# Loading the first block of a gated attention and feed-forward kernel: x tile by x tile, with the value products in the order of arrival

## The chip, the core and the metric

The kernel runs on one core of one Trainium2 chip. TensorE multiplies matrices (it loads a stationary operand, then streams a moving one), VectorE and ScalarE do the element work and empty PSUM, GpSimd writes constants, and SyncE (SP) issues most DMAs; ScalarE (ACT) issues two. The metric is the device time of one execution in microseconds (us), as the median of several runs. A profile of one execution gives the times inside it, counted from its first instruction (the span).

## The reference

```python
x = A_x                                                  # [1, 2048, 640], bf16
g = sigmoid((x * gate_w).sum(-1, keepdims=True))
# A: linear attention, 32 heads of 20
q, k, v = split_heads(x @ wqkv)                          # wqkv [640, 1920]
phi(t) = concat(softmax(t @ w_phi), softmax(-(t @ w_phi)))   # w_phi [32, 20, 20], per head
kv = phi(k)^T v ;  z = sum over tokens of phi(k)
a = (phi(q) kv / (phi(q) z + 1e-6)) @ wo                 # wo [640, 640]
# B: feed-forward
b = (gelu(x @ w_gate) * (x @ w_up)) @ w_down             # F = 1728
out = g * a + (1 - g) * b
```

## The kernel before, in words

The 2048 tokens are 16 tiles of 128; four tiles make a block. The 640 features are five slices (`KD = 5`) of 128 rows, which TensorE needs on the partitions, so everything begins with x transposed: `xT` holds it. Tiles 4 to 15 are transposed by DMA on their way in (`xturn`, L236). The first block goes another way, since it is wanted first: its tokens are loaded as they lie (`xload`, L229; tile j takes every fourth token, and two tiles come in one DMA of 320 KB), transposed on TensorE in 64-row halves through the identity (`x_transpose`, L333, with the transposes at L342), and copied out of PSUM into `xT` (L350 to L355: half of tile 3 on ScalarE and half on VectorE; tiles 0 and 2 whole on VectorE; tile 1 whole on ScalarE).

`attention_state` (L670) writes the order of work out by hand. It begins with nine products of constants (L674), warm-up that needs no data. Then come the transposes of tiles 0 and 1, six small filler products (L682), the transposes of tiles 2 and 3, and the values of the first block: `v_step(t, kt)` (L473) adds slice kt's share to the values of tile t, 640 columns in two products (480 in bank t, 160 in bank 4 or 5). For slice 0 the weights come in two DMAs (columns 0 to 255, then the rest; `VA = 256`), and the products are split in the same way. Slices 1 to 3 follow, each for all four tiles; then the block diagonals, the gate column, and slice 4, after which each tile's values are copied into `vaug` (`v_first_evac`, L484).

`blockdiag` (L357) spreads w_phi over `BD` in five VectorE instructions (L361); `BD` is later the moving operand of `fold` (L385), which multiplies w_phi into the key weights `wkT` and the query weights `wqT`. `gate_column` (L367) transposes the gate row `gz` on TensorE (L370) and VectorE copies it beside the value weights (L372); the first product that reads it is the second part of `v_tile(4, 2)`.

After the first values, three chunks of the up projection of block 0 are computed ahead (`up_ahead`, L546, products at L464), then the values of tiles 4 and 5, `fold` for the keys, the values of tiles 6 and 7, the keys of tile 0, two more up chunks, `fold` for the queries, and a loop over the tiles. The feed-forward part follows (`ffn`, L949).

The order of loads is fixed in `loads` (L222). SP issues, one after another: two x pairs, the value weights (two DMAs for slice 0, one of 160 KB for each further slice), the up weights of three chunks (`wue`, 480 KB), the DMA transposes of x tiles 4 and 5, of `wkT`, of x tiles 6 and 7, two more up chunks (`wul`), `wqT`, and x tiles 8 to 15 in two. ScalarE issues w_phi (25 KB, L276) after the second of GpSimd's masks, and the gate row (1.2 KB, L279). A helper, `_Sched`, sets the waits: an operation waits for the last writer of each tile it reads and for the readers of each it overwrites. Each engine works in program order.

Of the kernel before, what the change touches and what calls it, by code (L numbers as in the profile page):

```python
# [3 lines left out]
P = 128  # L4
BF16 = mybir.dt.bfloat16
F32 = mybir.dt.float32
AF = mybir.ActivationFunctionType
# [100 lines left out]
class _Kernel:  # L108
    S, D, H, DH, F = 2048, 640, 32, 20, 1728
    KD = D // P  # L110
# [111 lines left out]
    def loads(self):  # L222
        sc, nc = self.sc, self.nc
        D, KD, DH, P_ = self.D, self.KD, self.DH, P
        w3 = self.wqkv.rearrange("(kt p) n -> p kt n", p=P)

        x4 = self.x[0:self.BT, :].rearrange("(p j) n -> p j n", j=self.TB)

        def xload(q, j):  # L229
            sc.dma(q, lambda e: e.dma_start(self.xtok[:, j:j + 2, :], x4[:, j:j + 2, :]),  # L230
                   writes=[("xtok", j), ("xtok", j + 1)])

        def wload(T, c0, key):
            sc.dma("sp", lambda e: e.dma_start_transpose(T[:, :, :], self.wqkv[:, c0:c0 + D]), writes=[key])
# [1 line left out]
        def xturn(t, n):  # L236
# [5 lines left out]
              writes=["gtmp"])  # L242
        sc.op("pool", lambda e: e.memset(self.ident[:, :], 0.0), writes=["ident"])
        sc.op("pool", lambda e: e.affine_select(self.ident[:, :], self.ident[:, :], pattern=[[-1, P]],
                                                compare_op=ALU.not_equal, fill=1.0, base=0, channel_multiplier=1),
              writes=["ident"])
        xload("sp", 0)
        xload("sp", 2)
        for kt in range(KD):
            for a, z, key in ((0, self.VA, ("wv", 0)), (self.VA, D, "wv0")) if kt == 0 else ((0, D, ("wv", kt)),):  # L250
                sc.dma("sp", lambda e: e.dma_start(self.w3[:, kt, a:z], w3[:, kt, 2 * D + a:2 * D + z]), writes=[key])  # L251
        u3 = self.wu.rearrange("(kt p) n -> p kt n", p=P)
        a, z = self.UP[0] * P, 7 * P
        sc.dma("sp", lambda e: e.dma_start(self.wu_sb[:, :, a:z], u3[:, :, a:z]), writes=["wue"])
# [4 lines left out]
               writes=["wul"])  # L259
# [5 lines left out]
        for i in range(KD):  # L265
            n = self.HHI[i] - self.HLO[i] + 1
# [6 lines left out]
            pool(lambda e, m=m, n=n, base=base: e.affine_select(  # L273
                m, m, pattern=[[DH, n]], compare_op=ALU.is_ge, fill=0.0, base=DH - 1 - base, channel_multiplier=-1),
                [("mask", i)])
        sc.dma("act", lambda e: e.dma_start(  # L276
            self.wphi_sb[:, :, :], self.wphi.rearrange("h d f -> (h d) f").rearrange("(i p) f -> p i f", p=P)),
            reads=[("mask", 1)], writes=["wphi"])
        sc.dma("act", lambda e: e.dma_start(self.gz[0:KD, :], self.gw.rearrange("(k p) -> k p", p=P)), writes=["gz"])  # L279
        for r in (0, 1):  # L280
            m = self.hmask[:, r, :]
            pool(lambda e, m=m: e.memset(m, 1.0), [("hmask", r)])
# [47 lines left out]
            self.load(self.wd_sb[64 * r:64 * r + 64, 13, :], self.wd[13 * P:self.F, :], ("wd13", r))  # L330
        self.load(self.wo_sb[:, :, :], self.wo.rearrange("(kt p) n -> p kt n", p=P), "wo")

    def x_transpose(self, t, ek):  # L333

        sc = self.sc
        b, w = (0, 4, 2, 6)[t], self.D // 2
        bks = (b, b + 1)
        pv = self.bank(b, 1024).bitcast(BF16).rearrange("p (r c) -> p r c", r=2)[:, :, 0:w]
        for c in range(self.KD):
            for r in (0, 1):  # L340
                a = 64 * r
                sc.op("pe", lambda e: e.transpose(  # L342
                    pv[:, r, c * 64:(c + 1) * 64], self.xtok[a:a + 64, t, c * P:(c + 1) * P],
                    self.ident[a:a + 64, a:a + 64]),
                    reads=[("xtok", t), "ident"], writes=[("ps", bks[r])], signal=(c == self.KD - 1))
        out = self.xT[:, :, t * P:(t + 1) * P].rearrange("p c (r t) -> p c r t", t=64)
        src = pv.rearrange("p r (c t) -> p c r t", t=64)
        rd = [("ps", b) for b in bks]
        if ek == "ad":
            sc.op("act", lambda e: e.activation(out[:, :, 0, :], src[:, :, 0, :], AF.Copy), reads=rd[:1], writes=[("xh", t)])  # L350
            sc.op("dve", lambda e: e.tensor_copy(out[:, :, 1, :], src[:, :, 1, :]), reads=rd[1:], writes=[("xT", t)])
        elif ek == "a":
            sc.op("act", lambda e: e.activation(out, src, AF.Copy), reads=rd, writes=[("xT", t)])
        else:
            sc.op("dve", lambda e: e.tensor_copy(out, src), reads=rd, writes=[("xT", t)])  # L355

    def blockdiag(self):  # L357
        DH = self.DH
# [114 lines left out]
    def v_step(self, t, kt, part=None):  # L473
        sc = self.sc
        tail = (480, 160, 4 + t // 3, 160 * (t % 3))
        parts = ([(0, self.VA, t, 0)], [(self.VA, 480 - self.VA, t, self.VA), tail], [(0, 480, t, 0), tail])
        for c0, n, bk, col in parts[2 if part is None else part]:
            sc.op("pe", lambda e, c0=c0, n=n, bk=bk, col=col: e.matmul(  # L478
                self.bank(bk)[:, col:col + n], self.xT[:, kt, t * P:(t + 1) * P], self.w3[:, kt, c0:c0 + n],
                start=(kt == 0 and col == 0), stop=(kt == self.KD - 1), skip_group_check=True),  # L480
                reads=[("xT", t), ("xh", t), "wv0" if part == 1 else ("wv", kt)], writes=[("ps", bk)],
                signal=(kt == self.KD - 1))

    def v_first_evac(self, ts, ek, tail):  # L484
        sv, nt = ts[0], len(ts)
# [184 lines left out]
    def attention_state(self):  # L670
        NT = self.NT
        sc = self.sc
        ones = self.nc.const_aps.tensor(1.0, [P, 512], BF16)
        for n in (512, 512, 512, 512, 512, 512, 128, 128, 128):  # L674
            sc.op("pe", lambda e: e.matmul(self.bank(0, n), ones[:, 0:P], ones[:, 0:n], start=True, stop=True),
                  writes=[("ps", 0)])
        vs, ve, xt = self.v_step, self.v_first_evac, self.x_transpose
        xt(0, "d")
        xt(1, "a")
        for i in range(3):  # L680
            for a, b in ((0, 2), (64, 3)):
                sc.op("pe", lambda e: e.matmul(self.bank(b, P), ones[a:a + 64, 0:P], ones[a:a + 64, 0:P], start=True,  # L682
                                               stop=True), writes=[("ps", b)])
        xt(2, "d")
        xt(3, "ad")
        for t, part in ((0, 0), (1, 0), (0, 1), (1, 1), (2, 0), (2, 1), (3, 0), (3, 1)):
            vs(t, 0, part)
        for kt in range(1, 4):
            for t in range(4):
                vs(t, kt)  # L690
        self.blockdiag()
        self.gate_column(6)
        for t in range(4):
            vs(t, 4)
            ve([t], "ad"[t % 2], False)
            if t == 2:
                ve([0, 1, 2], "a", True)
        ve([3], "d", True)
        v, k, q = self.v_tile, self.k_tile, self.q_tile
        self.up_ahead(0, 7, "d")  # L700
        self.up_ahead(1, 6, "a")
        self.up_ahead(2, 4, "d")
        v(4, 2)
        self.v_split(5, 0)
        m, t, p = "main", "tail", "strip"
# [333 lines left out]
```

## Time and profile before

| what | value |
|---|---|
| median of 3 runs | 283.37 us (283.24 to 283.39) |
| span of the profiled execution | 282.4 us |
| TensorE busy | 278.6 us (99% of the span) |
| VectorE, ScalarE, GpSimd busy | 173.2, 105.9, 15.1 us |
| granted TensorE clock over the span | 1.000 |
| first transposes of x (L342) | 3.99 us |
| first value products (L478) | 5.37 us |
| first ahead-of-time up product (L464) | 11.53 us |

The time of a run is taken around the whole execution, while the span is from its first instruction to its last: the median stands 0.97 us above the span, and this difference is carried along. Busy time of TensorE counts pipelined products, whose ends are modelled. The chain that ended last is followed back from the last instruction: at each step to what released it, or to the instruction before it on its engine. "issue" is time in which an engine waited for nothing that the profile shows. In a timeline, neighbouring instructions of a line are merged into one row (start, length, engine, line, operation, output and inputs, count), and a bracket names the idle time ahead of them and what ended it; SPq and ACTq rows are DMA issues.

### The profile page before, as it was taken

Reading aid. Unit: us, or ns where it says so; the run is one execution under the profiler, and the core shown is the slowest. Engines: PE = TensorE matmul, PEld = TensorE weight load, DVE = VectorE, ACT = ScalarE, POOL = GpSimd, SP = SyncE. Lnnn points to the kernel's source line nnn. Section 1 sums busy time; section 2 is a strip of 40 time slices with the busy share of each in tenths; the row PEclk is TensorE's granted clock in tenths of the full one; section 3 lists DMA queues with packets and bytes.
Section 4 is the critical chain, followed back from the end, with each engine's and each line's share of the span. In section 5 each row is a group of like instructions: output and inputs, shape, how many; then the busy total and the mean of one; then the engine's idle time right before and its main releaser. Section 6 shows DMA issues by size and latency. Waiting matters only on the chain.

```text
span 282.4 us, 6904 instructions
## 1 busy us (share of the span) xinstructions
PE 278.6 (99%) x2926; PEld 168.6 (60%) x2926; DVE 173.2 (61%) x329; ACT 105.9 (38%) x204; POOL 15.1 (5%) x69
## 2 busy tenths in 40 slices
PE   7999999999999999999999999999999999999996
PEld 4566766665665444444444444445777777777786
DVE  1456999999997523694333324235883883883801
ACT  3246978777793332223232232321112112112011
POOL 7511001101000000000000000000000000000000
PEclk9999999999999999999999999999999999999999
DMA  7999169787789910011000000000133132532221
GB/s 213 193 223 190 29 127 172 153 175 149 157 175 274 350 51 0 2 24 23 2 0 0 0 2 0 0 0 2 26 50 98 46 49 78 66 49 73 73 72 49
DMA packets 60378, 24.11 MB, mean 85 GB/s; under 512 B 51002, under 2 KB 59834, under 8 KB 60346
## 3 DMA queue, kind: packets, MB, share of 16 engines
q1 hardware_dynamic: 59680, 23.63, 38.9%
q8 instruction: 23, 0.38, 0.6%
q10 hardware_dynamic: 666, 0.03, 0.2%
q14 instruction: 9, 0.07, 0.1%
HBM read 9.04 MB, written 2.62 MB: 41 GB/s over the span
## 4 chain that ended last, share of the span: by engine, by line
PE 97%; DMA 1%; SPq 0%; ACT 0%; issue 0%
PE ps L464 58%; PE ps L898 29%; PE ps L599 4%; PE ps L817 2%; PE ps L478 2%; PE ps L637 2%; DMA w<-in_A_wqkv_dram 1%; PE ps L404 1%; SPq L230 0%; SPq L251 0%; ACT outsb L911 0%; PE ps L370 0%
## 5 line engine op out<-in xcount | busy, mean ns | idle before, releaser
L464 PE MATMUL ps<-xT,wu_sb 128*128 128x512 bf16 x260 | 64.1, 379 | 0.0
L464 PE MATMUL ps<-xT,wg_sb 128*128 128x512 bf16 x260 | 63.9, 379 | 0.0
L779 ACT ACTIVATE gl<-ps 128x512 bf16<-128x512 f32 x52 | 31.0, 597 | 70.3 <-PE ps L464 70.3
L464 PE MATMUL ps<-w,xT 128*128 128x362 bf16 (+5 forms) x340 | 51.4, 302 | 0.0
L898 PE MATMUL ps<-wd_sb,hT 64*128 64x320 bf16 x648 | 48.4, 296 | 0.0
L781 DVE TENSOR_TENSOR hT<-ps,gl 128x512 bf16<-128x512 f32 x34 | 23.4, 689 | 37.7 <-PE ps L464 37.7
L464 PEld LDWEIGHTS ps<-xT,wu_sb 128*128 128x128 bf16 x260 | 25.4, 98 | 30.3 <-DVE hT L781 0.2
L464 PEld LDWEIGHTS ps<-xT,wg_sb 128*128 128x128 bf16 x260 | 25.1, 98 | 29.8 <-issue 0.2
L911 ACT ACTIVATE outsb<-ps,Gm 128x320 bf16<-128x320 f32 (+2 forms) x31 | 14.5, 515 | 71.8 <-PE ps L898 71.8
L464 PEld LDWEIGHTS ps<-w,xT 128*128 128x128 bf16 x340 | 31.9, 97 | 14.8
L898 PEld LDWEIGHTS ps<-wd_sb,hT 64*128 64x128 bf16 x648 | 30.9, 94 | 12.2 <-issue 0.4
L898 PE MATMUL ps<-wo_sb,goT 64*128 64x320 bf16 (+2 forms) x340 | 26.5, 288 | 0.0
L617 DVE TENSOR_REDUCE Dk<-Ek 128x66 f32<-128x1320 bf16 x16 | 24.3, 1520 | 2.3 <-ACT gcol L528 2.3
L626 DVE TENSOR_TENSOR Ek<-Ek,Dk 128x1320 bf16<-128x1320 bf16 x16 | 24.5, 1532 | 0.5
L863 DVE TENSOR_TENSOR O<-ps,RH 128x640 bf16<-128x640 f32 x32 | 24.7, 815 | 0.0
L538 ACT ACTIVATE Ek<-ps 128x627 bf16<-128x627 f32 x32 | 20.5, 693 | 6.4 <-PE ps L599 4.9
L538 ACT ACTIVATE Eqt<-ps 128x627 bf16<-128x627 f32 x32 | 20.6, 705 | 2.5 <-PE ps L464 2.5
L781 DVE TENSOR_TENSOR xT<-ps,gl 128x512 bf16<-128x512 f32 x13 | 9.0, 690 | 18.2 <-PE ps L464 18.2
L898 PEld LDWEIGHTS ps<-wo_sb,goT 64*128 64x128 bf16 x340 | 15.9, 94 | 5.3
L898 PE MATMUL ps<-wd_sb,xT 64*128 64x320 bf16 (+2 forms) x270 | 16.0, 269 | 0.0
L851 DVE RECIPROCAL RH<-ps 128x32 f32<-128x32 f32 x16 | 5.7, 357 | 14.4 <-PE ps L817 14.3
L898 PEld LDWEIGHTS ps<-wd_sb,xT 64*128 64x128 bf16 x270 | 12.1, 94 | 2.7
(90 smaller groups left out, 184.1 us busy)
## 6 DMA issues: line engine op xcount, KB each, us to landing
out_dram<-outsb SPq DMA_DIRECT2D x7, 320.0 KB, 2.3
wd_sb<-in_B_w_down_dram SPq DMA_DIRECT2D x1, 2080.0 KB, 11.0
wg_sb<-in_B_w_gate_dram SPq DMA_DIRECT2D x5, 224.0 KB, 3.1
wg_sb<-in_B_w_gate_dram SPq DMA_DIRECT2D x5, 192.0 KB, 3.5
wu_sb<-in_B_w_up_dram SPq DMA_DIRECT2D x5, 192.0 KB, 3.9
wo_sb<-in_A_wo_dram SPq DMA_DIRECT2D x1, 800.0 KB, 9.7
xtok<-in_A_x_dram SPq DMA_DIRECT2D x2, 320.0 KB, 3.3
w<-in_A_wqkv_dram SPq DMA_DIRECT2D x4, 160.0 KB, 4.0
```

The source lines that it names most:

```text
L464: self.sc.op("pe", lambda e: e.matmul(self.ps[:, bank * 512 + c0:bank * 512 + c0 + n], lhs, rhs, start=first, stop=fin), reads=reads, writ ...
L478: sc.op("pe", lambda e, c0=c0, n=n, bk=bk, col=col: e.matmul(self.bank(bk)[:, col:col + n], self.xT[:, kt, t * P:(t + 1) * P], self.w3[:, ...
L538: self.sc.op("act", lambda e: e.activation(dst, src, AF.Exp, scale=scale), reads=[("ps", b), ("ps", b + 1)], writes=[(name, sl, s)])
L599: self.sc.op("pe", lambda e: e.matmul(out, self.xT[:, kt, t * P:(t + 1) * P], self.w3[:, kt, c:c + 2 * n].rearrange("p (r w) -> p r w", w= ...
L617: self.sc.op("dve", lambda e: e.tensor_reduce(self.Dk[:, se, 0, :].rearrange("p (u h) -> p u h", h=self.HG), self.k_view(se), AX.X, ALU.ad ...
L626: sc.op("dve", lambda e: e.tensor_tensor(v, v, R.rearrange("p (u h) -> p u h", h=self.HG).unsqueeze(3).to_broadcast([P, 2 * self.G, self.H ...
L779: sc.op("act", lambda e: e.activation(self.gl[:, slot, :], self.bank(banks[0]), AF.Gelu_apprx_tanh), reads=[("ps", banks[0])], writes=[("g ...
L781: sc.op("dve", lambda e: e.tensor_tensor(hT, up, self.gl[:, slot, :], ALU.mult), reads=[upk, ("gl", slot)], writes=[("hT", hk, c)], guard=old)
L851: dve(lambda e: e.reciprocal(R(0), Dn[1]), rb, [key(0)], guard=old)
L863: dve(lambda e, o=o, f=f, s=s: e.tensor_tensor(o, V[s][:, :, 0:DH], f, ALU.mult), rb + [key(6 + s)], [("O", s, sl)], guard=old)
L898: sc.op("pe", lambda e: e.matmul(self.bank(bk, w), lhs, rhs, start=opens and x == 0, stop=end and not opens, skip_group_check=True), reads ...
L911: sc.op("act", lambda e: e.activation(dst, self.bank(bk, w), AF.Copy, scale=g), reads=rd, writes=wr)
```

## The change

The four x tiles are loaded singly, 160 KB each, in turn with the value weights of slices 0 to 3; slice 0 comes in one DMA. The value products are put in another order. Every tile is copied out of PSUM in halves, one on ScalarE and one on VectorE; the banks of the transposes, the number of warm-up and filler products, and one bank of an up chunk change. w_phi and the gate row are issued by ScalarE after tile 3's half copy, the gate row first. The block diagonals come after the value copies, and the gate column after the first up chunk.

```diff
         def xload(q, j):
-            sc.dma(q, lambda e: e.dma_start(self.xtok[:, j:j + 2, :], x4[:, j:j + 2, :]),
-                   writes=[("xtok", j), ("xtok", j + 1)])
+            sc.dma(q, lambda e: e.dma_start(self.xtok[:, j, :], x4[:, j, :]), writes=[("xtok", j)])
...
-        xload("sp", 0)
-        xload("sp", 2)
         for kt in range(KD):
-            for a, z, key in ((0, self.VA, ("wv", 0)), (self.VA, D, "wv0")) if kt == 0 else ((0, D, ("wv", kt)),):
-                sc.dma("sp", lambda e: e.dma_start(self.w3[:, kt, a:z], w3[:, kt, 2 * D + a:2 * D + z]), writes=[key])
+            if kt < self.TB:
+                xload("sp", kt)
+            sc.dma("sp", lambda e: e.dma_start(self.w3[:, kt, 0:D], w3[:, kt, 2 * D:3 * D]), writes=[("wv", kt)])
...
-        sc.dma("act", lambda e: e.dma_start(
-            self.wphi_sb[:, :, :], self.wphi.rearrange("h d f -> (h d) f").rearrange("(i p) f -> p i f", p=P)),
-            reads=[("mask", 1)], writes=["wphi"])
-        sc.dma("act", lambda e: e.dma_start(self.gz[0:KD, :], self.gw.rearrange("(k p) -> k p", p=P)), writes=["gz"])
...
-    def x_transpose(self, t, ek):
+    def x_transpose(self, t):
...
-        b, w = (0, 4, 2, 6)[t], self.D // 2
+        b, w = (6, 2, 6, 6)[t], self.D // 2
...
+        sc.op("act", lambda e: e.activation(out[:, :, 0, :], src[:, :, 0, :], AF.Copy), reads=rd[:1], writes=[("xh", t)])
+        sc.op("dve", lambda e: e.tensor_copy(out[:, :, 1, :], src[:, :, 1, :]), reads=rd[1:], writes=[("xT", t)])
+
+    def small_loads(self):
+        sc = self.sc
+        sc.dma("act", lambda e: e.dma_start(self.gz[0:self.KD, :], self.gw.rearrange("(k p) -> k p", p=P)), writes=["gz"])
+        sc.dma("act", lambda e: e.dma_start(
+            self.wphi_sb[:, :, :], self.wphi.rearrange("h d f -> (h d) f").rearrange("(i p) f -> p i f", p=P)),
+            writes=["wphi"])
...
+    def v_step(self, t, kt):
+        for c0, n, bk, col in ((0, 480, t, 0), (480, 160, 4 + t // 3, 160 * (t % 3))):
...
-        for n in (512, 512, 512, 512, 512, 512, 128, 128, 128):
+        for n in (512, 512, 512, 512, 512, 128, 128, 128, 128):
...
-        xt(0, "d")
-        xt(1, "a")
-        for i in range(3):
+        xt(0)
+        for i in range(4):
             for a, b in ((0, 2), (64, 3)):
...
-        xt(2, "d")
-        xt(3, "ad")
-        for t, part in ((0, 0), (1, 0), (0, 1), (1, 1), (2, 0), (2, 1), (3, 0), (3, 1)):
-            vs(t, 0, part)
-        for kt in range(1, 4):
-            for t in range(4):
-                vs(t, kt)
-        self.blockdiag()
-        self.gate_column(6)
+        vs(0, 0)
+        xt(1)
+        vs(0, 1)
+        xt(2)
+        for t, kt in ((1, 0), (1, 1), (0, 2), (1, 2)):
+            vs(t, kt)
+        xt(3)
+        self.small_loads()
+        for t, kt in ((2, 0), (2, 1), (2, 2), (0, 3), (1, 3), (2, 3), (3, 0), (3, 1), (3, 2), (3, 3)):
+            vs(t, kt)
         for t in range(4):
             vs(t, 4)
             ve([t], "ad"[t % 2], False)
             if t == 2:
                 ve([0, 1, 2], "a", True)
         ve([3], "d", True)
+        self.blockdiag()
         v, k, q = self.v_tile, self.k_tile, self.q_tile
         self.up_ahead(0, 7, "d")
-        self.up_ahead(1, 6, "a")
+        self.gate_column(6)
+        self.up_ahead(1, 0, "a")
         self.up_ahead(2, 4, "d")
```

More of the change, by code (lines that the diff above doesn't have):

```diff
@@ L348, in x_transpose @@
         rd = [("ps", b) for b in bks]
[L349 to L355, printed above, removed]
+        sc.op("act", lambda e: e.activation(out[:, :, 0, :], src[:, :, 0, :], AF.Copy), reads=rd[:1], writes=[("xh", t)])
[6 more added lines that the diff above has]
+            writes=["wphi"])
     def blockdiag(self):
@@ L471, in proj @@
                     kt == self.KD - 1, [("xT", t)] + [(k, kt) if k != "wgate" else k for k in keys])
[L473 to L478, printed above, removed]
+    def v_step(self, t, kt):
+        for c0, n, bk, col in ((0, 480, t, 0), (480, 160, 4 + t // 3, 160 * (t % 3))):
+            self.sc.op("pe", lambda e: e.matmul(
                 self.bank(bk)[:, col:col + n], self.xT[:, kt, t * P:(t + 1) * P], self.w3[:, kt, c0:c0 + n],
                 start=(kt == 0 and col == 0), stop=(kt == self.KD - 1), skip_group_check=True),
-                reads=[("xT", t), ("xh", t), "wv0" if part == 1 else ("wv", kt)], writes=[("ps", bk)],
-                signal=(kt == self.KD - 1))
+                reads=[("xT", t), ("xh", t), ("wv", kt)], writes=[("ps", bk)], signal=(kt == self.KD - 1))
     def v_first_evac(self, ts, ek, tail):
```

## The prediction

> **What bounds the kernel now.** I read the page first. TensorE is busy 278.6 of the 282.4 us span and carries 97% of the chain that ended last. The only other carriers of any size are the first loads. So I asked the chain, in order of time, for its first 20 us (start, length, what):
>
> ```profile
> 2.20 3.95 DMA w<-in_A_wqkv_dram
> 6.15 0.05 issue
> 6.19 4.35 PE ps L478 x34
> 10.54 0.06 PE ps L370
> 10.60 1.09 PE ps L478 x8
> 11.69 5.96 PE ps L464 x35
> ```
>
> See that TensorE waits last at 6.19, for a slice of the value weights. After that the chain is TensorE without a break to the last output (only 0.4 us of ScalarE stands at the end). Whatever brings the products of L478 forward therefore brings the end forward one for one, until something else comes late. Four steps of v_step take 1.09 us (10.60 to 11.69): 0.273 us each, of which there are 20. Then the timeline of the first 14 us:
>
> ```profile
> 2.85 0.43 ACTq L276 DMA_DIRECT2D wphi_sb<-in_A_w_phi_dram  x1
> ...
> 3.99 0.47 PE L342 MATMUL ps<-ident,xtok 64*128 64x64 bf16 x20
> ...
> 4.45 0.49 DVE L355 COPY xT<-ps 128x640 bf16<-128x640 bf16 x1 [4.45 <-PE ps L342]
> ...
> 5.05 3.77 SPq L238 DMA_TRANSPOSE xT<-in_A_x_dram  x1
> ...
> 5.27 0.44 ACT L350 ACTIVATE xT<-ps 128x320 bf16<-128x320 bf16 x1
> ...
> 8.86 4.78 SPq L234 DMA_TRANSPOSE wkT<-in_A_wqkv_dram  x1
> ```
>
> See the first tile's way: transposes at 3.99, the copy out of PSUM 0.46 later. And see that SP is inside two long transpose issues from 5.05 to 13.64. Last, the DMA issues (KB each, us from issue to landing):
>
> ```profile
> xtok<-in_A_x_dram SPq DMA_DIRECT2D x2, 320.0 KB, 3.3
> w<-in_A_wqkv_dram SPq DMA_DIRECT2D x4, 160.0 KB, 4.0
> wu_sb<-in_B_w_up_dram SPq DMA_DIRECT2D x1, 480.0 KB, 5.7
> ...
> wphi_sb<-in_A_w_phi_dram ACTq DMA_DIRECT2D x1, 25.0 KB, 4.5
> ```
>
> Asked for in narrow windows, the x pairs are issued at 0.80 and 1.27 and take 3.1 and 3.5 us: they land near 3.9 and 4.77. SP issues one load each 0.47 us ((5.05 - 0.80) / 9).
>
> **First term: when the first product can start.** The first pair (320 KB) is in at 3.94; the second follows 0.78 us later, so 160 KB are 0.39 us of flow. Half a pair first lands at 3.94 - 0.39 = 3.55. Bounds: 3.9, if size doesn't matter; 3.2, by the 64 KB loads of wu_sb (2.4 us after issue). I take 3.55, from the row of the same transfer. Then from the transposes' start: 0.46 to the copy (3.99 to 4.45), 0.44 for half a tile on ScalarE (L350; VectorE's half, 0.32, lies beside it), and some 0.1 to the product (a load's landing is followed by TensorE's work after 0.05 to 0.13). That is 1.0 us: products from 4.6. Before, the first two went at 5.37 and the unbroken run at 6.19.
>
> **Second term: what arrives next.** The nine loads alternate. Their pace lies between 0.39 us per 160 KB (the pairs) and 0.57 (the weight slices, landing at 6.57, 7.15, 7.72, with w_phi's 640-odd small packets among them). w_phi leaves this stretch, so I take 0.45: x1 at 4.45, weights 1 at 4.9, x2 5.35, weights 2 5.8, x3 6.25, weights 3 6.7, weights 4 7.15. TensorE in program order: (0,0) 4.6 to 4.87; tile 1 transposed to 5.02 (0.15 a tile, half of the 0.30 of two); (0,1) to 5.3; tile 2 to 5.5; then it waits for tile 1's copy, 4.87 + 1.0 = 5.87. From there 18 steps and one transpose, 18 x 0.273 + 0.15 = 5.06, with every load in time: the block ends at 10.93. With 0.57 a load, tile 2 comes at 5.83, the run starts at 6.03 and the end is 11.1. Before, the same block, with a gate column of 0.06 in it that is now paid later, ended at 11.53 (first product of L464), so at 11.47 without it. Gain 11.47 - 10.93 = 0.54; 0.35 at the slow pace. With the first landing's bounds it is 0.15 to 0.9.
>
> **Edits at nothing.** Warm-up: one 512-wide product goes (0.43 us) and a 128-wide comes (0.11), all ahead of 3.55. The two more fillers lie in the wait for tile 0's copy. Banks 6 and 7 are used three times; tile 3 needs tile 2's copy, done near 6.4, and starts near 6.85. The second up product's bank 0 needs the copy of tile 0's values, done near 11.0; it starts at 12.1. The block diagonals (5 x 0.30, laid 0.24 apart: 1.18 us of VectorE) move from an idle stretch to one with about 1.5 us idle between 13.5 and 15; covered, if w_phi is there.
>
> **What is late next on SP.** One load more puts up to 0.47 us on all behind it. The early up weights landed at 4.57 + 5.7 = 10.3, so by 10.75, needed at 10.93. wkT: 16.4, by 16.85, needed at 17.59 - 0.54 = 17.05. x tiles 6 and 7: 17.6, by 18.1, needed at 18.2. wqT: 23.4, by 23.9, needed at 24.5. All just in time, and a gain over 0.7 would meet them. The lower end is no shift at all: the first transpose issue took 3.77 us where one of the same size at 13.69 took 1.40, so over 2 us of it was waiting, in which 0.47 vanishes. I take a small shift and no stall. The Trainium skill ("DMA: Bandwidth & Descriptors", Rules for kernel authors) advises 1 MiB or more per DMA and so speaks against splitting; the rows say 0.39 us per 160 KB in pairs and 0.45 assumed here, so that rule would be worth 0.06 us a load, and by its side the sum is the 0.35 above.
>
> **What is late next on ScalarE.** The gate row and w_phi are now issued behind tile 3's half copy, near 7.3 to 7.8: 0.67 + 0.43 us of issue, done near 8.9. The landing: between 2.4 us (64 KB row) and 4.5 (w_phi's own row) after issue, so 10.8 to 13.0 for w_phi. Needed: the gate row at 12.0 by the gate column; w_phi by 12.9, since block diagonals 1.18, up copy 0.69 and gate copy 0.18 must be done on VectorE before the second part of v_tile(4) at 15.0. I take 12: no stall; at the late end 0.1.
>
> **Forecast:** 283.37 - 0.5 = 282.9 us. The span should go from 282.4 to 281.9; the 0.97 us between the span and the median stay. A difference under 0.2%, 0.57 us, is about what a measurement of this kernel can't tell from no change, so this is a gain at its edge. The case's own range is 282.4 to 283.2. Chance 0.62.
>
> **Rivals.**
> (1) *Slower: ScalarE stands behind SP's transposes.* No load in the trace is issued from ScalarE while SP is in a transpose; now two are. For it: SP's issues in that state stretch (3.77 against 1.40). Against: w_phi's issue at 2.85 overlapped SP's issues at 2.67 and 3.15, and all took 0.43. If each waits for a transpose issue to end: gate row after 9.3, wkT's issue 4.78 to 14.7, w_phi to 15.2. ScalarE's value copies stand behind it, so the second up product starts at 15.8 instead of 12.1, 3.7 late; w_phi lands near 17.2 and holds v_tile(4) another 0.4. 283.4 - 0.5 + 4.1 = 287.0. It decides once ScalarE is free later than about 11.5, each us costing a us. Chance 0.13. The Trainium skill ("Perfetto Trace Analysis", DMA Instruction — HWDGE) says that the descriptor generator is locked for exclusive use by one sequencer while it generates, which is this rival; the overlap at 2.85 shows no such lock for plain loads, and nothing here shows it for transposes.
> (2) *The small loads only land late*, their packets among the transposes' packets: w_phi at 13 to 14.5 holds v_tile(4), or the gate row holds the gate column, by 0.5 to 1.5: 283.4 to 284.4. Chance 0.11.
> (3) *The clock stays low longer.* The 512-wide warm-ups stand 0.43 apart (1.2 columns per ns); from 3.99 the ten pairs of 64-wide transposes of two tiles go by in 0.30, and the 512-wide up products later stand 0.216 apart (2.4). Warm-up is 0.32 us shorter, so busy time ahead of the change falls from 2.8 to 2.5 us. If the change is missed and comes the same 3.15 us later (0.84 to 3.99 once more), near 7.1, some six steps cost 0.27 more each, 1.6, less 0.4 of idle: 284.1. Chance 0.05.
> (4) *The gain is hidden:* the first half pair lands no earlier, or a transpose is late by half a us: 283.2 to 283.5. Chance 0.09.
>
> **Numbers.** Faster by over 0.2% needs a gain over 0.57, a little above my 0.5: 0.27 of the forecast's 0.62. Same: the other 0.35, 0.09 of (4), 0.02 of (2): 0.46. Slower: 0.13, 0.09 of (2), 0.05 of (3): 0.27. The range 282.4 to 284.4 takes in (2), (3) and (4) and leaves out (1) and some 0.04 below.
>
> **What would show it.** Right: transposes of tile 0 near 3.6, products from 4.6, unbroken from 5.9, first product of L464's up weights near 10.9, no wait of TensorE after it. Wrong: ScalarE's two issues longer than 0.5 and 0.7 us; TensorE waiting ahead of the gate column, of the second up product or of v_tile(4); a wait for wkT or x tiles 6 and 7; transposes of tile 0 after 3.8, or products at half rate.

## The result, and the profile after

| | before | changed |
|---|---|---|
| median | 283.37 us (283.11 to 283.91, 7 runs) | 284.65 us (284.22 to 284.8, 7 runs) |
| ratio to before, 95% interval | | 1.0036 [1.0026, 1.0047] |
| profiled execution: its own time, its span | not given, 282.4 | 284.65, 283.4 |
| first value product to first up product | 5.37 to 11.53 us | 4.46 to 11.87 us |
| first product of `fold` | 17.59 us | 18.56 us |

The change makes the kernel slower by 1.0 us as the ratio has it (1.3 between the medians). The forecast was 0.5 us the other way.

First the chain that ended last, of the changed kernel (start, length, what):

```profile
2.67 3.59 DMA xtok<-in_A_x_dram
...
8.13 5.34 DMA gz<-in_gate_w_dram
13.47 0.05 issue
13.51 0.23 PE ps L366
13.74 4.89 PE ps L460 x30
```

Before, one load stood in this chain. Now two do: the third x tile (landed 6.27) and the gate row, issued by ScalarE at 8.13 and landed only at 13.47, for which the gate column (L366) waits. On the page, the line of the chain by engine says the same for the whole span:

```profile
PE 95%; DMA 3%; SPq 1%; issue 0%; ACT 0%
```

TensorE had 97% before. Then the timeline of the changed kernel, from the first transposes to the gate column (start, length, engine, line; idle time ahead in brackets):

```profile
3.49 0.40 PE L336 MATMUL ps<-ident,xtok 64*128 64x64 bf16 x10
...
4.46 0.43 PE L471 MATMUL ps<-w,xT 128*128 128x480 bf16 x2 [0.34 <-ACT xT L343]
4.83 0.32 PE L336 MATMUL ps<-ident,xtok 64*128 64x64 bf16 x10
5.08 0.45 PE L471 MATMUL ps<-w,xT 128*128 128x480 bf16 x2
6.32 0.32 PE L336 MATMUL ps<-ident,xtok 64*128 64x64 bf16 x10 [0.79 <-DMA xtok<-in_A_x_dram]
6.57 1.27 PE L471 MATMUL ps<-w,xT 128*128 128x480 bf16 x8
7.77 0.32 PE L336 MATMUL ps<-ident,xtok 64*128 64x64 bf16 x10
8.02 4.01 PE L471 MATMUL ps<-w,xT 128*128 128x480 bf16 x28
8.13 0.56 ACTq L348 DMA_DIRECT2D gz<-in_gate_w_dram  x1
8.72 0.41 ACTq L349 DMA_DIRECT2D wphi_sb<-in_A_w_phi_dram  x1
...
11.87 1.24 PE L460 MATMUL ps<-xT,wu_sb 128*128 128x512 bf16 x5
13.51 0.23 PE L366 MATMUL ps<-ident,gz 128*128 128x128 bf16 x1 [0.41 <-DMA gz<-in_gate_w_dram]
```

The value block now begins 0.9 us earlier and ends 0.34 later. It takes 11.87 - 4.46 = 7.41 us, and this account closes on it: 20 steps of 0.273 are 5.46; three sets of transposes between products cost 0.35 each, 1.05 (from the first product at 4.46 to the one behind the transposes, at 5.08, are 0.62; one step of 0.27 lies between); the wait for the third x tile is 0.87 (0.79 in the bracket; step (0,1) and the row change behind it end near 5.45). Sum 7.38. Then the gate row: the first up chunk, 1.08 us of products, is through at 12.95, and the gate column begins at 13.51, 0.56 later. Behind the gate column TensorE waits for nothing more up to 60 us, and from the first product of `fold` to the end both kernels take 264.8 us: the whole loss lies ahead of `fold`.

From issue to landing the nine loads take 2.3, 2.7, 2.6, 2.6, 3.6, 3.9, 3.8, 3.9 and 4.7 us. With issues 0.47 us apart from 0.80 on they land at 3.10, 3.97, 4.33, 4.80, 6.27, 7.05, 7.42, 8.00 and 9.27: 0.77 us apart on average, in jumps.

### The profile page after: what moved, and what is told of

Same layout as the page of the kernel before. It is cut to its first block, busy times and chain, and to the rows that moved or that the text cites. A ratio compares the mean times of both kernels' runs of the same rounds, so it can differ in the third digit from the quotient of the medians.

```text
span 283.4 us, 6903 instructions
## 1 busy us (share of the span) xinstructions
PE 278.9 (98%) x2924; PEld 168.3 (59%) x2924; DVE 173.2 (61%) x330; ACT 106.6 (38%) x206; POOL 15.1 (5%) x69
## 4 chain that ended last, share of the span: by engine, by line
PE 95%; DMA 3%; SPq 1%; issue 0%; ACT 0%
PE ps L460 58%; PE ps L892 28%; PE ps L591 4%; PE ps L811 2%; PE ps L629 2%; DMA gz<-in_gate_w_dram 2%; DMA xtok<-in_A_x_dram 1%; PE ps L400 1%; PE ps L471 0%; SPq L249 0%; SPq L230 0%; PE ps L336 0%; ACT outsb L905 0%; PE ps L366 0%
```

## The experiments

Four explanations were open after this: the **gate row's late landing**; the **slow landing of single loads**; the **transposes among the products**; and the **profile of before** that the gain was counted against. Times below are medians (range, runs), each beside the runs of before on the same chip: set 1 283.45 (25 runs), set 2 283.29 (14), set 3 283.10 (20), set 4 283.28 (22).

### Set 1: the small loads, and the x tiles in pairs

**gate_row_early**: the changed kernel with the gate row issued at the start, where before issues it; w_phi stays late.

```diff
+        sc.dma("act", ... gz ...)          # in loads(), behind the masks
...
     def small_loads(self):
-        sc.dma("act", ... gz ...)
```

> The changed kernel with one edit: the gate row is issued by ScalarE at the start, ahead of the masks; w_phi stays behind tile 3's copy. Theory (two waits: the third x tile, landing at 6.27, costs the start of the run and leaves the value block 0.40 us later than before; the gate row, landing at 13.47, costs another 0.57): the wait ahead of L366 goes, w_phi still lands near 14 but holds nobody, so 0.57 less than the changed kernel, 283.7 to 284.1, still 0.3 to 0.6 above the kernel before. Rival (the late third tile is an accident of one profiled execution, the gate row alone is the loss): third tile lands by 5.4 to 5.8, value block ends 0.3 to 0.5 before the kernel before, 282.8 to 283.1.

Measured: 284.18 us (283.99 to 284.6, 8), ratio 1.0027 [1.0017, 1.0038], span 283.0. The wait ahead of the gate column is gone. From its chain:

```profile
7.95 6.30 DMA wphi_sb<-in_A_w_phi_dram
...
16.06 0.10 DVE w L368
...
16.20 2.06 PE ps L460 x15
```

What is late next is w_phi, which was expected to hold nobody: landed at 14.25, it pushes the block diagonals, the up copy (L546) and the gate copy (L368) on VectorE, and TensorE waits for that copy until 16.20 in `v_tile(4)`, some 0.4 us.

**small_loads_early**: both small loads back at before's place.

```diff
+        sc.dma("act", ... wphi ..., reads=[("mask", 1)], writes=["wphi"])     # in loads()
+        sc.dma("act", ... gz ...)
...
-        self.small_loads()
```

> The changed kernel with w_phi and the gate row issued where they were before the change (w_phi behind the second mask, then the gate row). Theory (two waits, and w_phi's small packets also take part in the early stretch): no wait ahead of L366; third x tile at 6.3 to 6.8, no earlier than in the changed kernel; total 283.8 to 284.3. Rival (w_phi's packets cost the early loads nothing, the lateness of the third tile was an accident): 282.8 to 283.2.

Measured: 284.18 us (283.84 to 286.06, 12; three of them at 285.78 to 286.06), 1.0039 [1.0022, 1.0056], span 282.8. No load is in the chain now:

```profile
5.66 0.65 PE ps L475 x2
...
8.06 3.94 PE ps L475 x28
12.01 1.08 PE ps L464 x5
13.09 0.06 PE ps L370
```

From the first up product on nothing waits, and the gate column takes its 0.06. But the value block ends no earlier: in the timeline the first up product is at 11.85, against 11.87 in the change. (The chain counts a product from where the one before it ends and has 12.01; before's first up product stands in the same way at 11.69 in the chain and at 11.53 in the timeline.) The two products of a step, with the change to the transposes behind them, take 0.65 here up to about 6.4 us, against 0.37 in the change (4.46 to 4.83): in this execution TensorE still runs at half rate then. So the small loads' late place explains a part of the loss, and some 0.7 us between the medians remain without it.

**before_small_loads_late**: the other side, before with the small loads, block diagonals, gate column and up chunk's bank moved as in the change.

```diff
         xt(3, "ad")
+        self.small_loads()
...
-        self.blockdiag()
-        self.gate_column(6)
...
+        self.blockdiag()
         self.up_ahead(0, 7, "d")
-        self.up_ahead(1, 6, "a")
+        self.gate_column(6)
+        self.up_ahead(1, 0, "a")
```

> The kernel before with the other half of the change alone: w_phi and gate row issued by ScalarE after tile 3's copy, block diagonals after the value copies, gate column after the first up chunk, the second up chunk in bank 0; x pairs, weights and product order as before. Theory (the gate row's packets come only when the transposed x tiles 4 and 5 have passed, near 13, whatever the start looks like): value block ends at or up to 0.3 before 11.47, TensorE then waits for the gate row until about 13, 0.3 to 0.7 us; total 283.4 to 284.0. Rival (the gate row was late only because it was issued at 8.1 behind the late third tile): issued near 5.8, it lands by 9, nobody waits, and without w_phi's packets the value block ends 0.2 to 0.4 earlier, 282.9 to 283.2.

Measured: 283.54 us (283.22 to 284.35, 12), 1.0007 [0.9998, 1.0016]. Here ScalarE is free at 5.48; the gate row lands at 10.89 and w_phi at 13.57, and nobody waits. (The transposes and the first products run at half rate in this profile, so that its first up product is at 11.53 although no load is late.) Two things follow. Moving w_phi out of the first loads' way brings nothing: the last value slice lands near 8.0, as in before's second profile (below). And a later place is harmless here, where the issue comes 2.6 us earlier than in the change.

**pairs_gate_row_early**: the changed kernel with the x tiles as two pairs ahead of the weights, and the gate row early.

```diff
+        xload("sp", 0)                     # pairs, as before
+        xload("sp", 2)
         for kt in range(KD):
-            if kt < self.TB:
-                xload("sp", kt)
```

> As the kernel with the gate row early, and the x tiles are loaded in two pairs ahead of the weights again (as before the change, but the first weight slice in one DMA); the products keep the new order. Theory (single tiles in turn put the third x tile into a stretch near 5 to 6 us where loads land late, and every later product in program order waits for it): the pairs land at 3.9 and 4.8, first weights near 5.2, products from 5.3, the run is held by weights 1 and 2 at most, the first up product near 11.3 to 11.5, total within 0.2 us of the kernel before, 283.2 to 283.6, and 0.3 to 0.6 under the kernel with single tiles and gate row early. Rival (loads in turn are harmless, the order of products is what costs): no better than the kernel with single tiles, first up product at 11.8.

Measured: 285.64 us (284.09 to 286.35, 6), 1.0068 [1.0042, 1.0094]; three runs at 286.1 and more, two at 284.09 and 284.24. The first weights land at 5.29, the products start at 5.42 and stay at half rate until 8.86, and w_phi, landed at 16.14, holds `v_tile(4)`. It doesn't tell how pairs do, since these two cover that.

### Set 2: the order and the warm-up

**pairs_in_turn**: pairs, but in turn with the weights (pair, weights 0, pair, weights 1 to 4); small loads early; six 512-wide warm-up products. The products behind the transposes follow in the order in which this brings their operands, and tile 3 is transposed through another bank.

```diff
         for kt in range(KD):
-            if kt < self.TB:
-                xload("sp", kt)
+            if kt < 2:
+                xload("sp", 2 * kt)
...
         xt(0)
+        xt(1)
...
         vs(0, 0)
-        xt(1)
-        vs(0, 1)
         xt(2)
-        for t, kt in ((1, 0), (1, 1), (0, 2), (1, 2)):
-            vs(t, kt)
+        vs(1, 0)
         xt(3)
...
```

> First pair of x tiles, all of weight slice 0, second pair, then slices 1 to 4; products: (tile 0, slice 0), tile 2 transposed, (1,0), tile 3 transposed, then as they can run; all copies in halves; w_phi and gate row early as before the change; warm-up of the kernel before (six 512-wide). Theory (what costs in the changed kernel is the single tiles' slow pace, some 0.7 us a load, the wait for the small loads, and a short warm-up; the order of products is sound): pair 1 at 3.9, slice 0 near 4.6, pair 2 near 5.4, products from 5.0 with under 0.4 us of waits, first up product near 11.1 to 11.3 (11.47 before, without the gate column): 283.0 to 283.4. Rival (any product order that starts early only meets later loads): first up product at 11.5 or later, 283.4 to 283.9.

Measured: 284.33 us (283.44 to 286.06, 8), 1.0039 [1.0022, 1.0056], span 282.7. The first pair lands at 3.68, the first weights at 4.06, and products start at 4.62; the second pair lands at 5.85 and costs a wait of 0.84. Both expectations (at most 283.9) are missed: here too the load behind the first tiles and weights is late, 1.8 us after them.

**mended_order**: the changed kernel with the small loads early, six warm-up products, and tile 2 transposed after steps (1,0) and (1,1).

```diff
         vs(0, 1)
+        for t, kt in ((1, 0), (1, 1)):
+            vs(t, kt)
         xt(2)
-        for t, kt in ((1, 0), (1, 1), (0, 2), (1, 2)):
+        for t, kt in ((0, 2), (1, 2)):
             vs(t, kt)
```

> The changed kernel with the small loads early, the warm-up of the kernel before, and tile 2 transposed only after the products (1,0) and (1,1), so that a third tile that lands near 6 holds nobody. Theory (the wait for the third tile is the first loss): no wait of over 0.2 us at the transposes of tile 2; first up product 11.4 to 11.7; 283.4 to 283.8, and no runs near 286. Rival (the loads' pace as a whole binds, wherever the waits are put): the wait moves to the next load, first up product 11.7 or later, 283.8 to 284.2.

Measured: 284.13 us (283.95 to 284.49, 5), 1.0032 [1.002, 1.0044], span 282.9. Products at full rate from 4.83, one wait (0.2 to 0.4 us, for tile 1's copy, at 6.19), no late load. The first up product is still only near 11.9 (its weight load is at 11.79) and `fold` at 17.98. This order hides the loads nearly whole and does not win either.

**changed_warm_longer** and **changed_warm_shorter**: the changed kernel with more and with less warm-up.

```diff
-        for n in (512, 512, 512, 512, 512, 128, 128, 128, 128):
+        for n in (512, 512, 512, 512, 512, 512, 512, 128):       # longer
+        for n in (512, 512, 512, 128, 128, 128, 128):            # shorter
```

> The changed kernel with a longer warm-up: seven 512-wide products and one 128-wide, so TensorE is busy until about 3.9 instead of 3.45. Theory (the changed kernel's time is set by the third tile and the gate row, the clock rises near 3.7 in most of its runs): same as the changed kernel, 284.3 to 284.8. Rival (in part of its runs the clock rises one period, 3.4 us, later, as in the two kernels of the first set whose first record stood at 6.4 and 8.9): 0.3 or more below it, 283.8 to 284.2, and less scatter.

Measured: 284.79 us (284.39 to 285.07, 5), 1.0053 [1.004, 1.0066], span 283.5. No half rate among the value products, and as slow as the change. The third x tile is in time in this execution, and the weight load of the first up product stands 0.35 us earlier than in the change (11.45 against 11.80); but the gate row lands at 13.59 all the same, and the 0.35 are lost in a longer wait for it (0.88 in the bracket).

> The changed kernel with a shorter warm-up: three 512-wide and four 128-wide products, TensorE busy until 2.6. [...] Rival (the rise comes a fixed time after the first product of constants): near 3.7 to 4.1 as in the changed kernel, 284.3 to 284.8.

Measured: 286.86 us (284.62 to 288.76, 6; five at 286.58 or more), 1.0125 [1.0092, 1.0158], span 285.3. Its timeline, to be held against the changed kernel's rows above:

```profile
6.71 2.31 PE L471 MATMUL ps<-w,xT 128*128 128x480 bf16 x8
8.96 0.45 PE L336 MATMUL ps<-ident,xtok 64*128 64x64 bf16 x10
```

The eight products that took 1.20 us (6.57 to 7.77) take 2.25 (6.71 to 8.96). The half rate lasts to about 9.55, so the rise doesn't come a fixed time after the first product of constants (that would be near 4); w_phi, issued later with everything else, lands at 16.53 and holds `v_tile(4)` 1.08.

### Set 3: one price at a time

**three_switches**: before, with a pair of 64-row products of constants after the second step of slices 1, 2 and 3. They compute nothing that is used.

```diff
                 vs(t, kt)
+                if t == 1:
+                    for a, b in ((0, 6), (64, 7)):
+                        sc.op("pe", ... e.matmul(self.bank(b, P), ones[a:a + 64, 0:P], ones[a:a + 64, 0:P], ...
```

> The kernel before with three pairs of 64-row products of constants put into the unbroken run of value products, one pair in each of slices 1 to 3. Theory (each change between 128-row and 64-row products costs 0.09 us, twice a pair, and the pair itself 0.06): first up product 0.7 later, 0.6 to 0.8 above the kernel before. Rival (the 0.09 seen in the changed kernel belongs to its waits, not to the change of rows): 0.1 to 0.25 above.

Measured: 283.84 us (283.73 to 284.14, 8), 1.0027 [1.0017, 1.0037]: 0.76 us. Its chain:

```profile
7.18 0.16 PE ps L693 x2
7.34 1.20 PE ps L478 x8
8.55 0.16 PE ps L693 x2
```

Eight products of an unbroken run take 1.09 (10.60 to 11.69 in the prediction's first fence). With a change of rows behind them they take 1.20, and the pair's own piece is 0.16. So a break costs 0.11 + 0.16 = 0.27. The work in it is small: its two products are 128 wide, and four times that width stand 0.216 apart (the 512-wide up products), so 0.054 is an estimate for 128 columns; the eight filler pairs of first_slice_whole_busy (below) take 0.47 in its chain, 0.06 a pair. The two changes of rows make up the rest, some 0.1 each if they share it evenly. An interruption as such does not cost this: the gate column (L370), one product of 128 rows and 128 columns between value products, takes 0.06 in the prediction's first fence.

**before_x_single**: before, with the x tiles loaded singly ahead of the weights.

```diff
-        xload("sp", 0)
-        xload("sp", 2)
+        for j in range(self.TB):
+            xload("sp", j)                 # one tile, 160 KB
```

> The kernel before with the x tiles loaded singly, the four of them ahead of the weights; nothing else changed. Theory (single x tiles, pieces of 1280 bytes, flow more slowly than pairs, 0.6 to 0.7 us a tile against 0.4): fourth tile near 5.1 to 5.4 instead of 4.73, later slices 0.4 to 0.6 later, first up product 11.8 to 12.1, 283.6 to 284.0. Rival (it is the alternation of x and weights that is slow, not the single tile): fourth tile by 4.9, 283.2 to 283.5.

Measured: 283.84 us (283.69 to 284.21, 7), 1.0025 [1.0014, 1.0036]: 0.7 us, span 282.5. From its chain:

```profile
3.15 3.06 DMA w<-in_A_wqkv_dram
```

The x tiles land at 3.12, 3.53, 4.89 and 5.32. Slice 0's second part, sixth in the queue and not fourth, lands at 6.20; before's second profile (below) has it at 5.47.

**first_slice_whole**: before, with slice 0 in one DMA and its products unsplit.

```diff
-            for a, z, key in ((0, self.VA, ("wv", 0)), (self.VA, D, "wv0")) if kt == 0 else ((0, D, ("wv", kt)),):
-                sc.dma("sp", lambda e: e.dma_start(self.w3[:, kt, a:z], ...
+            sc.dma("sp", lambda e: e.dma_start(self.w3[:, kt, 0:D], ...
...
-        for t, part in ((0, 0), (1, 0), (0, 1), (1, 1), (2, 0), (2, 1), (3, 0), (3, 1)):
-            vs(t, 0, part)
-        for kt in range(1, 4):
+        for kt in range(4):
```

> The kernel before with one edit: weight slice 0 comes in one 160 KB DMA instead of 64 and 96 KB, and its products are not split. Theory (the kernel before waits at 5.75 for the second part of slice 0, which lands at 6.15 in small pieces; a whole slice behind the x pairs landed at 5.29 in the kernel with pairs): products from 5.4 without a break, first up product near 11.0, 0.3 to 0.6 under the kernel before, 282.7 to 283.0. Rival (w_phi's packets slow the whole slice as they did the parts): slice 0 at 5.6 to 5.9, 283.0 to 283.3.

Measured: 283.32 us (282.91 to 283.93, 11), 1.0003 [0.9994, 1.0012]. Products run unbroken from 5.36; `fold` begins at 17.01. It is before's equal, where 0.3 to 0.6 us under it were expected.

**first_slice_whole_busy**: the same with more filler products (eight and five pairs) and a longer warm-up.

```diff
-        for i in range(3):
+        for i in range(8):
...
         xt(3, "ad")
+        for i in range(5):
+            for a, b in ((0, 0), (64, 1)):
+                sc.op("pe", ... ones ...)
```

> As first_slice_whole, and TensorE is kept busy with constants until the first products: seven 512-wide warm-ups and one 128-wide, sixteen fillers after tile 1's transposes and ten after tile 3's. [...] Rival (with six warm-ups the clock is in time in nearly all runs): the same, or up to 0.15 higher from the fillers.

Measured: 284.16 us (283.36 to 284.28, 5), 1.0039 [1.0026, 1.0053]. The profiled run is the one at 283.36; the other four are at 284.14 and above, far more than the 0.15 us expected of the fillers, and no trace shows why.

### Set 4: a second issuer, and both kernels once more

**two_queues**: small_loads_early, with the weights of slices 0 to 2 issued by ScalarE beside SP's x tiles. (Here and in first_slice_two_queues ScalarE's DMAs also get eight semaphores in place of four.)

```diff
+        for j in range(self.TB):
+            xload("sp", j)
         for kt in range(KD):
-            if kt < self.TB:
-                xload("sp", kt)
-            sc.dma("sp", ...
+            sc.dma("act" if kt < 3 else "sp", ...
```

> The kernel small_loads_early with the loads issued from two engines: the four x tiles, then weight slices 3 and 4 and all else from SP, slices 0 to 2 from ScalarE (then w_phi and the gate row). Theory A (the single loads' pace is set by SP, which issues one 160 KB load each 0.47 us): all of them issued by 3.6, third x tile by 5.0, slice 3 near 6.5 instead of 8.0, first up product near 11.0, 283.1 to 283.5. Theory B (the flow itself is slow in this stretch, whoever issues): third tile still at 5.6 to 6.3, slice 3 at 7.4 to 8.0, first up product 11.5 to 11.9, 283.8 to 284.2.

Measured: 283.69 us (283.54 to 285.47, 12), 1.002 [1.0007, 1.0033], span 282.5. The nine loads land between 3.83 and 7.58, 0.47 apart, where the change's stood 0.77 apart and those of small_loads_early 0.67. So the issue by SP alone, 0.47 us a load, does set part of the pace. The time lies between its two expectations. With nearly every load in time the chain has no wait of note from 4.89 on:

```profile
5.96 0.25 PE ps L341 x10
6.21 1.24 PE ps L476 x8
7.44 0.25 PE ps L341 x10
7.70 3.94 PE ps L476 x28
11.64 0.05 issue
```

and still the value block ends only at 11.64, 0.5 us behind the 11.14 in the chain of before's second profile (below). This is the change's order with its loads mended. Its products begin 0.52 us earlier (4.89 against 5.41), and three sets of transposes stand between them, 1.05.

**first_slice_two_queues**: first_slice_whole, with slices 0 and 1 issued by ScalarE.

```diff
+            sc.dma("act" if kt < 2 else "sp", ...
```

> The kernel first_slice_whole (x pairs first, slice 0 whole) with slices 0 and 1 issued from ScalarE. Theory A (issue sets the pace): slice 0 lands 0.3 to 0.5 sooner, by 4.9, products from 5.2 (tile 0's copy and the transposes bound them), 0.1 to 0.2 below first_slice_whole. Theory B (the flow sets it): slice 0 shares the stretch with the second x pair, which lands later by what slice 0 gains; same as first_slice_whole or up to 0.3 above.

Measured: 283.96 us (283.64 to 285.94, 12; four at 285.56 to 285.94), 1.0035 [1.001, 1.0059]. Weights 0 land early (4.51), but at the pairs' cost: 4.34 and 5.60. What the weights won the second pair lost (4.69 in before's second profile), and products start at 6.04.

**changed_again** and **before_again**: both kernels unchanged, for a second profile of each.

> The changed kernel once more, unchanged, for a second profiled execution beside the kernel before on the same chip. Theory (third tile late and gate row late are of this kernel, not of one execution): third tile at 5.7 to 6.3, wait ahead of L366 of 0.4 to 1.0, 1.0 to 1.4 above the kernel before. Rival (the landing of the third tile at 6.27 was an accident): third tile by 5.4, and the difference 0.5 to 0.8.

Measured: 285.04 us (284.45 to 287.07, 6), 1.0069 [1.0043, 1.0094], span 283.7. Gate row 13.75, wait 0.81; products at half rate until about 5.9. The long gap between loads, 1.7 us, stands ahead of the second x tile here, and the third lands at 6.04. The loss to before is 2.0 us by the ratio, more than expected.

> The kernel before once more, unchanged, for a second profiled execution. Theory (its first profiled execution, with the second part of slice 0 at 6.15, was slower than its typical run): the second part of slice 0 at 5.4 to 5.8, unbroken run from 5.5 to 5.8, first up product 11.0 to 11.3, span 281.7 to 282.2. Rival (the first one was typical): 6.0 to 6.3, 11.4 to 11.6, 282.3 to 282.5.

Measured: 283.22 us, span 281.9. Its chain:

```profile
5.47 4.52 PE ps L478 x36
...
10.05 1.09 PE ps L478 x8
...
11.20 5.91 PE ps L464 x34
```

Hold this against the prediction's first fence: there TensorE waits until 6.19 for a slice; here there is no wait, since the slice landed at 5.47 and not at 6.15. The value products end at 11.14 (10.05 + 1.09), not 11.69, and `fold` begins at 17.11, not 17.66 (in the chains): 0.55 us earlier, both. The row at 11.20 needs care. It holds 34 products where before's has 35 (fifteen up products and the twenty for the values of tiles 4 and 5): the record of the first up product is missing, as the row of TensorE's weight loads shows:

```profile
10.91 2.11 PEld L464 LDWEIGHTS ps<-xT,wu_sb 128*128 128x128 bf16 x11
```

In before's first profile the weight load stands at 11.46 and the product at 11.53. So the first up product of the second profile is put at 10.98, an estimate, and the product at 11.20 is the next, 0.22 behind it. Over all 81 runs of before in the four sets the median span is 282.0 us; 17 of them reach the 282.4 of the first profile. Time less span is 1.29 us in the median.

## Why the prediction was wrong, point by point

**The baseline failed first.** The gain of 0.54 us was counted from a block that ended at 11.47 without its gate column. That execution had met a late slice. In before's second profile the first up product is at 10.98, and at 10.92 without the gate column. Against that, the prediction's own end, 10.93, is worth nothing, and not 0.54: the gain was the late slice of one execution. The offset of 0.97 was a sign of it that couldn't be read with one profile: it set the span of one execution against the median of others, and within one execution it is 1.29.

**First term: right in time, but not by its own path.** Transposes at 3.49 and not 3.6, products at 4.46 and not 4.6. The first tile landed at 3.10: below the 3.55 taken, and 0.1 below the lower end. It then waited for TensorE, whose warm-up products run up to the transposes; with less of them (changed_warm_shorter) the transposes start at 3.09. So it is luck that the term came so close.

**Second term, the pace of the loads: failed.** Taken 0.45 us a load, bounds 0.39 to 0.57; measured 0.77 on average, with a jump of 1.47 ahead of the third x tile, for which TensorE waited 0.87. The first bound came from loads of 320 KB, each with one issue for twice the bytes. Single x tiles alone cost before 0.7 us (before_x_single). A second issuer brings the pace to 0.47 (two_queues), so the issue on SP sets part of it. w_phi's leaving, which was the reason for 0.45, brought nothing (before_small_loads_late; and with w_phi back in its early place, small_loads_early, the pace is 0.67). The rule of the Trainium skill that spoke against splitting ("DMA: Bandwidth & Descriptors", Rules for kernel authors) pointed the right way, and was priced at 0.06 us a load; the rows give 0.3.

**Transposes among the products: failed in its price.** 0.15 us a tile was half of two tiles' transposes that stand together. Between products a set costs 0.35, and three_switches shows why: a change from 128-row to 64-row products and back costs some 0.2, over and above the work between. Three sets at 0.2 us above their price are 0.6, as much as the whole gain that was forecast. The Trainium skill has the mechanism ("TensorEngine Tiling (Array Packing)", Key Properties): changing the tiling mode drains TensorE. It gives no figure, and the prediction didn't weigh it; the runs here agree with it, at some 0.1 us a change.

**Late next on ScalarE: failed, and this was rival (2).** The gate row was to be in by 12.0 and landed at 13.47, 13.59 and 13.75 in three executions. It wasn't the issue: ScalarE's two took 0.56 and 0.41 us while SP was inside a transpose issue, so rival (1) fell. The DMA queues of the changed kernel, from 8.2 to 11.2 us and from 11.2 to 11.9 (packets, MB, share), show where it was:

```profile
q1 hardware_dynamic: 1642, 0.66, 113.7%
...
q10 hardware_dynamic: 617, 0.03, 60.6%
```

ScalarE's queue (q10) moves nothing for 3 us after its first issue, while SP's (q1) moves 1642 packets; then it moves nearly all of its packets in half a us, and still the landing is seen only at 13.47, after a stretch with next to no packets; x tiles 4 and 5, in transpose by DMA since 5.53, land at 13.9. What holds it at each of these two places the runs don't show. w_phi lands at 13.9 as well; in all seven profiles where it was issued behind a DMA transpose it landed within 0.3 us of the landing of one. The gate row did so less strictly: 0.3 to 0.5 ahead of x tiles 4 and 5 in the three executions above, but 2.9 ahead of them in before_small_loads_late (10.89 against 13.8). The bounds of 2.4 and 4.5 us came from loads with no DMA transpose ahead of them. Moved early, the gate row costs nothing, w_phi is next with 0.4 (gate_row_early), and with both early neither waits (small_loads_early).

**Late next on SP: right.** No product waits for the early up weights, `wkT`, or x tiles 6 and 7.

**Rival (3), the clock:** not in the profile of the change, where the first two value products take 0.37 with the row change behind them. But it is near: changed_again and small_loads_early run their first products at half rate, and with less warm-up that lasts to 9.55 and the median is 2.2 us above the change's, the late w_phi (1.08) included. The row of the granted clock doesn't show it (1.000 in each profile); the products' distances do. The Trainium skill ("TensorE: Matmul & The Clock Gate", Part 1) has a free-running window of 3.4 us that must be busy. That such executions come and go without an edit agrees with it; its figure of under 1% of the span for the penalty isn't passed here (2.2 of 284 us).

**The sum, corrected.** Against before's second profile: the block ends 0.89 us later (11.87 against 10.98), TensorE waits 0.56 for the gate row, and the gate column, 0.07 from its start to the next product's, now stands behind the block. That is 1.52, and `fold` begins 1.52 later (18.56 against 17.04 in the timelines); the spans differ by 1.5 (283.4 - 281.9). Against the prediction's own span of 281.9 the miss is the same 1.5: transposes 0.6, the wait for the third tile 0.5 more than the 0.37 it had for tile 1's copy, the gate row 0.56, less 0.14 for the earlier start. These parts can't be won back one by one: TensorE goes on behind the gate row at 13.5 to 13.8 in all three executions, though in one of them (changed_warm_longer) the block ends 0.35 earlier. So as built the gate row's landing sets the time, and the rest shows only when it is moved. Had every load been in time, the block would have ended at 4.46 + 5.46 + 1.05 = 10.97, where before has 10.98 with its gate column: the change had nothing to win, as in rival (4), though for another reason. The range that was stated ended at 284.4, since it took each rival alone and rival (2) on top of the gain; here the gain failed and rival (2) came as well.

**A version that beats both** wasn't found. first_slice_whole equals before; all other edits are slower or within the bound of no change. Open: why single loads flow in jumps near 4 to 6 us beyond what their issue explains, what holds the small loads at 11.7 to 13.5, and why four runs of first_slice_whole_busy are above 284.1.

## What to carry to other kernels

A wait for a first load, seen in one profiled execution, is a draw and not a size: look at the spread of spans, or at a second profile, before a gain is counted from it. When a dense run of products is broken to let work in as it arrives, price each change between whole-row and half-row products, not only the work let in. And a small load moved behind a DMA transpose should be counted to land about when that transpose does, however few its bytes: here 25 KB always did, and 1.2 KB in most executions.

## What was not expected of the hardware

- A pair of 64-row products between 128-row products costs 0.27 us (0.76 for three), although a pair takes some 0.06 among its like; a 128-row product of that width in the same place takes 0.06.
- Nine loads of 160 KB from one issuer landed 0.77 us apart in the change (0.67 with w_phi early), from two issuers 0.47.
- A load of 1.2 KB took 5.3 us to land where DMA transposes were under way, and none of its queue's packets moved in the first 3 us.
- The fourth load of before (96 KB) landed at 6.15 in one execution and at 5.47 in another, and the end of the kernel moved with it, by 0.5 us.
